# Loading a small residual in its final layout, and x in one transfer, in a single-core decode step

## The chip, the core and the metric

The kernel runs on one core of a Trainium2 chip. The metric is the device time of one execution in microseconds (us). A core has five engines that work side by side: TensorE (PE in the profile, with its weight loads as PEld), VectorE (DVE), ScalarE (ACT), GpSimd (POOL) and SyncE (SP). Each has its own queue of instructions, which it works off in order. Transfers between the memories are carried out by 16 DMA engines; an instruction on SP's or ACT's queue issues a transfer and is done, and a semaphore says later that the data have landed.

## What is computed

One decode step: a layer norm of x, grouped-query attention over the last 1024 cached positions, a gated feed-forward network on the same normalised x, and a residual.

```python
x = A_x                                   # (8, 1, 512) bf16: 8 sequences, one token each
xn = layernorm(x)
q = (xn @ wq)                             # 32 heads of 128; 8 key/value heads
p = softmax(q @ k_window.T * 128**-0.5)   # k_window, v_window: last 1024 of 4096 positions
s = (p @ v_window) @ wo                   # (8, 1, 512)
g = silu((gelu(xn @ w_gate) * (xn @ w_up)) @ w_down)
return x + s * g
```

Every key, value and weight is used once: per sequence 2 MB of keys and 2 MB of values, then 4 MB of wq, three feed-forward matrices of 1792 KB each and 4 MB of wo, all in bf16.

## The kernel before

All work is in one function, written so that each engine runs its instructions in the order of the text. The big transfers are all issued from SP: keys of sequence 0 (line 73, two transfers of 1 MB), wq (line 94, two of 2 MB), then keys and values of the other sequences in the order in which they are used, the feed-forward weights (lines 423 and 426) and wo (line 437), whose last megabyte is cut into pieces of 640, 256 and 128 KB. They land in a ring of eight slots of 4 MB, 32 KB per partition, so that SP runs ahead of the computation.

The start of the computation is the layer norm of x. x_sb holds the eight rows of x on eight partitions. It is loaded by four transfers of two rows each, issued from ACT (line 68). DVE takes the statistics (lines 129 and 131), ACT the square root (line 133), DVE the reciprocal and xhat (lines 134 and 136). TensorE turns xhat (line 151), and DVE writes the result four times into xnR (line 153), whose 32 columns per block hold the eight sequences at every fourth place. xnR is the stationary operand of the q projection (line 248) and, later, of the feed-forward matmuls (line 451).

The residual is needed at the very end, in the layout of the output: 128 partitions in four blocks of 32, block t with columns 128t to 128t + 127 of x, and inside a block the sequence b on partition 4b (RB = 4). To bring x into that layout, POOL builds a padded identity xpad (lines 116 and 117), TensorE multiplies it with the four column blocks of x_sb (line 156), and ACT copies the result from PSUM into x_res (line 163), which is fp32. After that ACT does nothing until the q projection has finished, when it copies q out of PSUM (line 258).

Then DVE turns keys (line 235), TensorE forms scores (line 296), DVE and ACT do the softmax (lines 306 to 318), TensorE the values (line 340), for one sequence after the other. At the end come the feed-forward network (lines 451 to 492) and the output projection (line 499), which runs as the pieces of wo land; DVE multiplies by the gate (y, line 507), adds x_res (out_sb, line 509), and SP stores the result (line 511).

The framework counts landed transfers on eight semaphores. The trace names the semaphore of each transfer: the eight are used in turn over SP's and ACT's transfers together, and a transfer that uses one again waits for the earlier transfer on it to land. So at most eight transfers are under way. SP's instruction waits where it stands, and all that SP issues after it waits behind it.

Of the kernel before, what the change touches and what calls it, by code (L numbers as in the profile page):

```python
# [8 lines left out]
ALU = mybir.AluOpType  # L9
AX = mybir.AxisListType  # L10
BF16 = mybir.dt.bfloat16
FP32 = mybir.dt.float32
# [4 lines left out]
RB = 4  # L17
# [4 lines left out]
def kernel(  # L22
# [13 lines left out]
    nc = tc.nc  # L36

    B, Sq, D = A_x.shape
# [7 lines left out]
    P = nc.NUM_PARTITIONS  # L46
# [7 lines left out]
    DT = D // 4  # L54
# [3 lines left out]
    keep = ctx.enter_context(tc.tile_pool(name="keep", bufs=1))  # L58
# [3 lines left out]
    def slot(name):  # L62
        return ring.tile([P, 2 * ROW], BF16, name=name, tag="slot")


    x_sb = keep.tile([B, D], BF16, name="x_sb")
    for r in range(0, B, 2):
        nc.scalar.dma_start(out=x_sb[r : r + 2], in_=A_x.flatten_outer_dims()[r : r + 2])

    def load_cache(cache, b, name):  # L70
        t = slot(name).rearrange("p (g x) -> p g x", g=NG)
# [20 lines left out]
    for i in range(2):  # L92
        t = slot("wq_sb").rearrange("p (k n) -> p k n", k=NK // 2)
# [9 lines left out]
        out=ident,  # L103
        in_=ident,
        compare_op=ALU.not_equal,
        fill=1.0,
        base=0,
        pattern=[[-1, P]],
        channel_multiplier=1,
# [2 lines left out]
    nc.vector.memset(eps_sb, 1e-5)  # L112
    xnR = keep.tile([P, NK, 4, 32], BF16, name="xnR")
    nc.vector.memset(xnR, 0.0)
    xpad = keep.tile([B, 32], BF16, name="xpad")
    nc.gpsimd.memset(xpad, 0.0)
    nc.gpsimd.affine_select(
        out=xpad,
        in_=xpad,
        compare_op=ALU.not_equal,  # L120
        fill=1.0,
        base=0,
        pattern=[[-1, 32]],
        channel_multiplier=RB,
    )


    stats = keep.tile([B, nc.vector.BN_STATS_DIM], FP32, name="stats")
    nc.vector.bn_stats(out=stats, in_=x_sb)  # L129
    mv = keep.tile([B, nc.vector.BN_AGGR_DIM], FP32, name="mv")  # L130
# [6 lines left out]
        out=xhat,  # L137
# [3 lines left out]
        op0=ALU.subtract,  # L141
        op1=ALU.mult,
    )
    x_res = keep.tile([P, DT], FP32, name="x_res")
    warm = keep.tile([B, 1], FP32, name="warm")
    nc.scalar.activation(out=warm, in_=rstd, func=ACT.Exp)
    with tc.tile_pool(name="ps_x", bufs=1, space=PSUM) as ps_x:
        xnT_ps = ps_x.tile([P, NK, B], BF16, name="xnT_ps")
        xv = xhat.rearrange("b (p k) -> b k p", k=NK)
        for k in range(NK):  # L150
            nc.tensor.transpose(xnT_ps[:, k, :], xv[:, k, :], ident[0:B, 0:B])  # L151
        for j in range(4):
            nc.vector.tensor_copy(out=xnR[:, :, j, 0 : RB * B : RB], in_=xnT_ps)
        xr_ps = ps_x.tile([P, DT], FP32, name="xr_ps")
        for t in range(4):
            nc.tensor.matmul(
                xr_ps[32 * t : 32 * t + 32, :],
                xpad,
                x_sb[:, t * DT : (t + 1) * DT],
                start=True,  # L160
                stop=True,
            )
        nc.scalar.copy(out=x_res, in_=xr_ps)

    qd = Hq // NG
    neg_st = consts.tile([P, 4, Hq], BF16, name="neg_st")
# [5 lines left out]
        out=hv,  # L174
        in_=hv,
        compare_op=ALU.not_equal,
        fill=0.0,
        base=0,
        pattern=[[0, 4 * NG], [-1, HG], [0, rep]],
        channel_multiplier=1,  # L180
    )
    nc.gpsimd.affine_select(
        out=neg_st,
        in_=neg_st,
        compare_op=ALU.is_ge,
        fill=0.0,
        base=HG - 1,
        pattern=[[0, 4 * Hq]],
        channel_multiplier=-1,
# [3 lines left out]
        out=neg_mv,  # L193
        in_=neg_mv,
        compare_op=ALU.not_equal,
        fill=1.0,
        base=0,
        pattern=[[0, 512 // HG], [-1, HG]],
        channel_multiplier=1,
# [7 lines left out]
    for g in range(NG):  # L207
        nc.vector.tensor_reduce(
            out=sel[:, g, g * qd : (g + 1) * qd],
            in_=ident.rearrange("p (t g h) -> p g h t", t=4, g=NG)[:, g],  # L210
# [5 lines left out]
        out=own, in_=ident.rearrange("p (i e) -> p e i", e=8), axis=AX.X, op=ALU.add  # L216
    )
    pick = consts.tile([P, 4 * NU], BF16, name="pick")
    with nc.allow_low_precision(reason="sums of zeros and a single one"):
        nc.vector.tensor_reduce(  # L220
            out=pick, in_=ident.rearrange("p (a e) -> p a e", e=8), axis=AX.X, op=ALU.add
# [22 lines left out]
    with tc.tile_pool(name="ps_q", bufs=1, space=PSUM) as ps_q:  # L244
        q_ps = [ps_q.tile([P, 512], FP32, name=f"q_ps{i}") for i in range(8)]
        for k in range(NK):
            for i in range(8):
# [4 lines left out]
                    start=(k == 0),  # L252
                    stop=(k == NK - 1),
# [174 lines left out]
    for u in range(NU):  # L428
        if u % 2 == 0:
            pair = slot("wo_sb").rearrange("p (v j d) -> p v j d", v=2, d=D)  # L430
        t = pair[:, u % 2]
# [15 lines left out]
    for n, ws in (("z_ps", wgu[0]), ("u_ps", wgu[1])):  # L447
        ps = ps_f.tile([P, FT], FP32, name=n)
        for k in range(NK):
            for t in range(4):  # L450
# [4 lines left out]
                    start=(k == 0),  # L455
                    stop=(k == NK - 1),
# [6 lines left out]
        out=z2, in0=z2, scalar1=0.044715, scalar2=1.0, op0=ALU.mult, op1=ALU.add  # L463
# [11 lines left out]
        out=hT.rearrange("p j b -> p (j b)"), in_=h_bf.rearrange("p (y j) -> p j y", j=NJ)  # L475
    )
    f_ps = ps_f.tile([P, DT], FP32, name="f_ps")
    for j in range(NJ):
        for t in range(4):
# [4 lines left out]
                start=(j == 0),  # L484
                stop=(j == NJ - 1),
# [4 lines left out]
        out=g_sb, in0=g_sb, scalar1=0.5, scalar2=0.5, op0=ALU.mult, op1=ALU.add  # L490
# [5 lines left out]
    for u in range(NU):  # L496
        for j in range(8):
            for t in range(4):
# [4 lines left out]
                    start=(u == 0 and j == 0),  # L503
                    stop=(u == NU - 1 and j == 7),
# [7 lines left out]
        out=out_f.rearrange("b (t d) -> t b d", t=4), in_=out_sb[0 : P : RB, :]  # L512
# [31 lines left out]
```

## Time and profile before

| What | Value |
|---|---|
| median of 3 runs | 121.49 us (121.39 to 121.63) |
| the profiled execution | 121.48 us, of which its span is 119.4 us |
| PE, DVE, ACT, POOL busy | 73.0, 75.8, 31.4, 3.2 us |
| mean granted TensorE clock | 0.838 |
| read from memory over the span | 47.46 MB, mean 399 GB/s with the write |
| DMA queue of SP (q1) | 6228 packets, 47.46 MB, 94.3% of 16 engines' span |
| DMA queue of ACT (q10) | 16 packets, 0.01 MB, 0.0% |
| idle of DVE until x has landed | 5.7 us |
| idle of ACT until q is ready (line 258) | 12.2 us |

The profile is one execution, seen by the hardware. The span runs from the first instruction to the last; what lies between it and the time of the run, some 2.1 us here, is before and after the program. The page cuts the span into 40 slices of about 3 us and gives the busy share of each engine and of the DMA engines in each. Beside the page, the trace has every instruction with its semaphores and every packet that a DMA engine moved, with its start, duration and size. Most packets of the large transfers are 8192 bytes and take 309 ns.

### The profile page before, as it was taken

To read this page: it belongs to the slowest core of one execution; us is meant where nothing else is said; L and a number is where in the kernel's file an instruction comes from. 1 tells how busy PE (TensorE), PEld (TensorE's weight loads), DVE (VectorE), ACT (ScalarE), POOL (GpSimd) and SP (SyncE) were. 2 spreads that over 40 slices of the span, in tenths; PEclk is the share of its full clock that TensorE was granted. 3 is DMA by queue.
4 is the path that set the end of the run, shared out by engine and by line. 5 is a ranking of instruction groups with operands and counts; after the bars stand their busy time and mean duration, and the time that the engine had idled before them with its cause. 6 is when DMAs were issued, how large, how long until landed. Compare 5 with 4: busy or idle time off the path is not lost.

```text
span 119.4 us, 2300 instructions
## 1 busy us (share of the span) xinstructions
PE 73.0 (61%) x985; PEld 38.7 (32%) x992; DVE 75.8 (63%) x101; ACT 31.4 (26%) x75; POOL 3.2 (3%) x10
## 2 busy tenths in 40 slices
PE   0001499811994987969687674991994547545370
PEld 0000134300341544535443351450453433143350
DVE  1048978399739999999959959909943241651000
ACT  2233000676007052341712510700616211200000
POOL 2006100000000000000000000000000000000000
PEclk9999999985599999999999998599589855555555
DMA  1999999999999999999999999999999999999930
GB/s 47 411 445 417 434 425 431 417 428 434 428 420 425 431 423 423 428 423 431 417 431 420 431 423 423 428 428 423 420 434 439 437 433 418 427 421 417 412 148 3
DMA packets 6254, 47.61 MB, mean 399 GB/s; under 512 B 732, under 2 KB 868, under 8 KB 1124
## 3 DMA queue, kind: packets, MB, share of 16 engines
q1 hardware_dynamic: 6228, 47.46, 94.3%
q8 instruction: 8, 0.13, 0.4%
q10 hardware_dynamic: 16, 0.01, 0.0%
q14 instruction: 2, 0.02, 0.0%
HBM read 47.46 MB, written 0.01 MB: 397 GB/s over the span
## 4 chain that ended last, share of the span: by engine, by line
DMA 85%; DVE 6%; PE 4%; SPq 2%; issue 1%
DMA k_sb<-in_A_k_cache_dram 48%; DMA wo_sb<-in_A_wo_dram 20%; DMA v_sb<-in_A_v_cache_dram 17%; DVE kT L235 4%; PE S_ps L296 2%; PE s_ps L499 1%; SPq L73 1%; DVE mx L306 1%; SPq L94 1%; PE O_ps L340 1%; PE r_ps L389 1%; DVE y L507 0%; DVE out_sb L509 0%; DVE oT L392 0%; DVE m L311 0%
## 5 line engine op out<-in xcount | busy, mean ns | idle before, releaser
L296 PE MATMUL S_ps<-kT,qbd 128*128 128x512 bf16 x128 | 34.1, 413 | 15.5 <-DVE kT L235 11.9
L235 DVE STREAM_TRANSPOSE kT<-k_sb 128x2048 int32<-128x2048 int32 x16 | 36.5, 2289 | 4.4 <-DMA k_sb<-in_A_k_cache_dram 4.3
L296 PEld LDWEIGHTS <-qbd 128*128 128x128 bf16 x128 | 12.8, 102 | 31.9 <-issue 16.4
L248 PE MATMUL q_ps<-wq_sb,xnR 128*128 128x512 bf16 x32 | 9.8, 481 | 4.3 <-DMA wq_sb<-in_A_wq_dram 4.3
L316 ACT ACTIVATE nb<-m 32x1 f32<-32x1 f32 x32 | 6.4, 201 | 22.5 <-DVE m L313 22.2
L306 DVE TENSOR_REDUCE mx<-S_ps 128x1 f32<-128x1024 f32 x8 | 9.6, 1196 | 4.1 <-PE S_ps L296 4.1
L318 ACT ACTIVATE P_sb<-S_ps,nb 128x1024 bf16<-128x1024 f32 x8 | 11.1, 1390 | 0.3
L340 PE MATMUL O_ps<-v_sb,pT 128*32 128x128 bf16 x512 | 9.1, 226 | 2.6 <-DVE pT L329 2.6
L340 PEld LDWEIGHTS <-pT 128*32 128x32 bf16 x512 | 7.6, 100 | 5.6 <-issue 3.0
L353 ACT COPY O_sb<-O_ps 128x256 f32<-128x256 f32 x8 | 3.0, 372 | 23.3 <-PE O_ps L340 23.3
L329 DVE STREAM_TRANSPOSE pT<-P_sb 128x512 int32<-128x512 int32 x8 | 5.7, 711 | 3.4 <-ACT P_sb L318 3.3
L248 PEld LDWEIGHTS <-xnR 128*128 128x128 bf16 x32 | 3.7, 118 | 10.1 <-issue 8.1
L361 PE MATMUL o_ps<-O_sb,sel 128*32 128x128 f32 x32 | 6.3, 332 | 0.9 <-ACT O_sb L353 0.9
L499 PE MATMUL s_ps<-wo_sb,oT 128*32 128x128 bf16 x128 | 4.4, 307 | 3.7 <-DMA wo_sb<-in_A_wo_dram 3.7
L258 ACT CAST q_both<-q_ps 128x512 bf16<-128x512 f32 x6 | 3.0, 611 | 12.2 <-PE q_ps L248 12.2
L151 PE MATMUL xnT_ps<-ident,xhat 8*128 8x8 bf16 x4 | 0.3, 174 | 8.9 <-DVE xhat L136 8.9
L499 PEld LDWEIGHTS <-oT 128*32 128x32 bf16 x128 | 3.5, 136 | 4.7 <-issue 4.5
L361 PEld LDWEIGHTS o_ps<-O_sb,sel 128*32 128x32 f32 x32 | 3.4, 128 | 5.0 <-issue 1.7
L507 DVE TENSOR_TENSOR y<-s_ps,g_sb 128x128 f32<-128x128 f32 x1 | 0.3, 292 | 7.2 <-PE s_ps L499 7.2
L285 PE MATMUL S_ps<-neg_mv,neg_st 128*128 128x512 bf16 x9 | 3.3, 384 | 1.9 <-DVE q_both L258 1.9
L129 DVE BATCH_NORM_STATS2 stats<-x_sb 8x6 f32<-8x512 bf16 x1 | 0.7, 681 | 5.7 <-DMA x_sb<-in_A_x_dram 5.7
L240 DVE MEMSET qbd<- 128x4096 uint32 x1 | 3.5, 3472 | 0.8 <-issue 0.8
(64 smaller groups left out, 51.2 us busy)
## 6 DMA issues: line engine op xcount, KB each, us to landing
k_sb<-in_A_k_cache_dram SPq DMA_DIRECT2D x16, 1024.0 KB, 19.7
v_sb<-in_A_v_cache_dram SPq DMA_DIRECT2D x16, 1024.0 KB, 20.0
wq_sb<-in_A_wq_dram SPq DMA_DIRECT2D x2, 2048.0 KB, 11.4
wo_sb<-in_A_wo_dram SPq DMA_DIRECT2D x3, 1024.0 KB, 25.1
wgu_sb<-in_B_w_gate_dram SPq DMA_DIRECT2D x1, 1792.0 KB, 21.4
wgu_sb<-in_B_w_up_dram SPq DMA_DIRECT2D x1, 1792.0 KB
wd_sb<-in_B_w_down_dram SPq DMA_DIRECT2D x1, 1792.0 KB
wo_sb<-in_A_wo_dram SPq DMA_DIRECT2D x1, 640.0 KB
```

Of the source, the lines that this page charges most:

```text
L235: nc.vector.transpose(out=t.bitcast(I32), in_=k_sb[b][:, g].bitcast(I32))
L240: nc.vector.memset(qbd, 0.0)
L248: nc.tensor.matmul(q_ps[i], xnR[:, k, :, :].rearrange("p j b -> p (j b)"), wq_sb[k][:, i * 512 : (i + 1) * 512], start=(k == 0), stop=(k = ...
L285: nc.tensor.matmul(S[b][:, half, :], neg_st.rearrange("p j h -> p (j h)"), neg_mv.rearrange("p a n -> p (a n)"), start=True, stop=False,)
L296: nc.tensor.matmul(S[b][:, half, :], qbd[:, m, b, w, g, :], kv[:, half * 16 : (half + 1) * 16, m, :, w], start=False, stop=(g == NG - 1 an ...
L306: nc.vector.tensor_reduce(out=mx, in_=S[b].rearrange("p a c -> p (a c)"), axis=AX.X, op=ALU.max)
L316: nc.scalar.mul(nb[32 * j : 32 * j + 32, :], m1, -inv)
L318: nc.scalar.activation(out=P_sb[b].rearrange("p c i w -> p c w i"), in_=S[b].rearrange("p a (c w i) -> p (a c) w i", w=2, i=32), func=ACT.Exp,
L329: nc.vector.transpose(out=pT[b].rearrange("p c h w -> p (c h w)").bitcast(I32), in_=P_sb[b].rearrange("p c i w -> p (c i w)").bitcast(I32),)
L340: nc.tensor.matmul(O_ps[b][32 * t : 32 * t + 32, g, :], pT[b][:, c // 2, :, c % 2], vv[:, c, :], start=(c < 4), stop=(c >= C - 4),)
L361: nc.tensor.matmul(o[:, 0:Dh], sel[:, g, :], O_sb[b][:, g, :], start=(g == 0), stop=(g == NG - 1))
L499: nc.tensor.matmul(s_ps[32 * t : 32 * t + 32, :], oT[:, j, u, :], wo[u][:, j, t * DT : (t + 1) * DT], start=(u == 0 and j == 0), stop=(u = ...
```

## The change

x is loaded in one transfer of eight rows. xpad, the four matmuls with it and ACT's copy are gone. x_res is now bf16; POOL fills it with zeros, and three transfers issued from ACT, after the activation `warm`, write x into it straight from memory: one of column blocks 0 and 1 (16 rows of 256 bytes), one of block 2 and one of block 3 (8 rows of 256 bytes each). DVE's addition at the end reads a bf16 operand in place of an fp32 one. Before and after there are four small transfers from ACT.

```diff
     x_sb = keep.tile([B, D], BF16, name="x_sb")
-    for r in range(0, B, 2):
-        nc.scalar.dma_start(out=x_sb[r : r + 2], in_=A_x.flatten_outer_dims()[r : r + 2])
+    nc.scalar.dma_start(out=x_sb, in_=A_x.flatten_outer_dims())
...
-    xpad = keep.tile([B, 32], BF16, name="xpad")
-    nc.gpsimd.memset(xpad, 0.0)
-    nc.gpsimd.affine_select(
-        out=xpad,
...
-        pattern=[[-1, 32]],
-        channel_multiplier=RB,
-    )
...
-    x_res = keep.tile([P, DT], FP32, name="x_res")
+    x_res = keep.tile([P, DT], BF16, name="x_res")
+    nc.gpsimd.memset(x_res, 0.0)
     warm = keep.tile([B, 1], FP32, name="warm")
     nc.scalar.activation(out=warm, in_=rstd, func=ACT.Exp)
...
-        xr_ps = ps_x.tile([P, DT], FP32, name="xr_ps")
-        for t in range(4):
-            nc.tensor.matmul(
-                xr_ps[32 * t : 32 * t + 32, :],
-                xpad,
-                x_sb[:, t * DT : (t + 1) * DT],
-                start=True,
-                stop=True,
-            )
-        nc.scalar.copy(out=x_res, in_=xr_ps)
+    x_t = A_x.flatten_outer_dims().rearrange("b (t d) -> t b d", t=4)
+    for a, z in ((0, 2), (2, 3), (3, 4)):
+        nc.scalar.dma_start(out=x_res[32 * a : 32 * z : RB, :], in_=x_t[a:z])
```

More of the change, by code (lines that the diff above doesn't have):

```diff
@@ L114 @@
     nc.vector.memset(xnR, 0.0)
-    xpad = keep.tile([B, 32], BF16, name="xpad")
-    nc.gpsimd.memset(xpad, 0.0)
-    nc.gpsimd.affine_select(
-        out=xpad,
[L119 to L122, printed above, removed]
-        pattern=[[-1, 32]],
-        channel_multiplier=RB,
-    )
     stats = keep.tile([B, nc.vector.BN_STATS_DIM], FP32, name="stats")
```

## The prediction

> **What bounds the kernel now.** I read the page's slices first.
>
> ```profile
> DMA  1999999999999999999999999999999999999930
> GB/s 47 411 445 417 434 425 431 417 428 434 428 420 425 431 423 423 428 423 431 417 431 420 431 423 423 428 428 423 420 434 439 437 433 418 427 421 417 412 148 3
> ```
>
> The DMA engines are full in every slice but the first and the last two, at some 425 GB/s, while no compute engine is over 63% busy. Second, the chain of waits in order of time, its end:
>
> ```profile
> 70.88 19.86 DMA v_sb<-in_A_v_cache_dram
> ...
> 90.76 24.04 DMA wo_sb<-in_A_wo_dram
> ...
> 114.84 1.28 PE s_ps L499 x28
> ...
> 116.15 0.30 DVE y L507
> ...
> 116.47 0.29 DVE out_sb L509
> ```
>
> Transfers make 85% of that chain; after the last one come a few matmuls, two DVE instructions and the store. Third, does SP ever issue too late? The waits of SP's queue:
>
> ```profile
> SPq L73 <- DMA k_sb<-in_A_k_cache_dram: 25.3, 13, 2.3
> SPq L73 <- DMA v_sb<-in_A_v_cache_dram: 19.2, 10, 2.5
> SPq L73 <- DMA wq_sb<-in_A_wq_dram: 8.5, 2, 4.3
> SPq L73 <- DVE oT L392: 0.3, 1, 0.3
> ```
>
> SP waits for earlier transfers to land (eight semaphores, eight transfers under way), and for compute once, 0.3 us, with some 20 us of transfers queued ahead. So the time is: when the stream starts, how long the slowest DMA engine needs, and the tail. From the packet records: the first key packet starts at 2.52 us, the last wo packet ends at 115.47, the last matmuls start at 115.80, out_sb ends at 116.76, the store lands at 118.26 and the span ends at 119.4. Fourth, the start, in the timeline:
>
> ```profile
> 0.80 1.54 ACTq L68 DMA_DIRECT2D x_sb<-in_A_x_dram  x4
> 0.80 1.30 SPq L73 DMA_DIRECT2D k_sb<-in_A_k_cache_dram  x2
> ...
> 7.02 0.68 DVE L129 BATCH_NORM_STATS2 stats<-x_sb 8x6 f32<-8x512 bf16 x1 [5.71 <-DMA x_sb<-in_A_x_dram]
> ...
> 9.13 0.29 PE L156 MATMUL xr_ps<-x_sb,xpad 8*32 8x128 bf16 x4
> 9.23 0.52 DVE L153 COPY xnR<-xnT_ps 128x32 bf16<-128x32 bf16 x4 [0.38 <-PE xnT_ps L151]
> ...
> 9.65 0.24 ACT L163 COPY x_res<-xr_ps 128x128 f32<-128x128 f32 x1
> ...
> 13.71 0.58 PE L248 MATMUL q_ps<-wq_sb,xnR 128*128 128x512 bf16 x1 [4.29 <-DMA wq_sb<-in_A_wq_dram]
> ```
>
> x is late (7.02), but xnR is ready at 9.75 and the q projection starts at 13.71, when wq lands. The layer norm has 3.96 us to spare.
>
> **x in one transfer.** The first of the four x transfers, issued at 0.80, ran its packets at 1.74 and 1.79, before any key packet, and its semaphore was full at 2.34. The other three waited behind key packets (starts 3.69 to 6.17). One transfer in the first one's place should land near 2.4, some 4.5 us earlier; three issues (0.24, 0.40 and 0.28 us of ACT) go. Statistics, xhat and xnR move up to about 5 us, and DVE's first key transposes from 11.68 to some 8.1, when the first keys have landed. What hides all of it is the 4.29 us wait for wq. Value: 0. A gain of 4.5 us would need that wait to go; the transfer that it waits for does not move.
>
> **The matmuls, xpad and the copy.** 0.29 us of PE, 0.24 of ACT, 0.12 and 0.21 of POOL, all before 9.9 us and all under the same wait: 0. The zeroing of x_res is a POOL memset, between 0.10 us (the constant memsets) and DVE's 0.17 for a 128x128 bf16 tile, on a POOL that idles 8.2 us after that: 0.
>
> **ACT's three new issues.** At 0.24 to 0.54 us each (the four at line 68) they take 0.7 to 1.6 us, from about 5.2 us on. Behind them on ACT is the copy of q, for which ACT sat idle 12.2 us until 22.09. Eight semaphores go round over both queues, so an issue of ACT can also wait for an earlier transfer. Four small transfers before, four after: later in the kernel the turn is as it was. SP, which had to wait for the x transfers' semaphores (its issues at 3.33, 6.80, 7.45 and 8.11), will stand instead on a wq or x_res transfer until about 13 or 18 us; 9 or 10 MB have been issued by then and 4 or 5 are still to come (2.45 us each MB, so 10 us or more), and the stream does not run dry. If ACT is held until wq has landed (SP was held so until 13.59 and 18.42), q's copy is still in time. Value 0; up to 3.7 us late (a wait for values landing near 25.8) it is still covered, since the first slot that depends on it, that of the values of sequence 0, was refilled at 46.4 and free some 4.8 us earlier.
>
> **The packets in the stream.** This is the only place where microseconds can come from. Packets on one DMA engine run one after the other: each x row took 46 ns and each semaphore write 9, and the next key packet started right behind. The engines do not end together. By the ends of the wq transfers (12.55 to 13.23) they are up to 0.68 us apart, and these offsets stay to the end, except where an instruction fetch of 16 KB runs on one engine, which sets it back by 1.42. The last engine is one with 0.37 at the start and a fetch at 83.4: 1.79. The two engines with x packets stand at 0.11 and 0.15; the first gets a fetch and ends at 1.52. So the x packets that go, 3 x (46 + 9) = 0.17 us on each, are not on the engine that ends last: 0, in bounds of 0 to -0.17. The x_res packets: if block 0-1 goes to two engines as the pairs of x rows did, each takes 8 packets, and one or two more of the other transfers. The nearest row is the store of the output, 32 packets of 256 bytes at 15 to 18 ns: 10 x 18 + 3 x 9 = 0.21, against the 0.17 that goes: 1.56, still under 1.79. On other engines up to 2 x (18 + 9) = 0.05. I take +0.05. The bound above is the 60 ns of the slowest x row in the stream: 10 x 60 + 27 - 165 = 0.46 more, 1.98, which is 0.19 over 1.79.
>
> [...] The x rows in the trace held their engine for some 46 ns, so the sum here counts packets alone.
>
> **The start of the stream.** The windows by stage:
>
> ```profile
> 2.70:5.20 2.50, 0.00 (x0) 0.00 (x0) 0.00 (x0) 0.95 (x1) 0.00 (x0) 1.00 0.89 368
> 5.20:7.70 2.50, 0.00 (x0) 0.00 (x0) 0.68 (x1) 0.00 (x0) 0.00 (x0) 1.00 1.04 437
> 30.00:60.00 30.00, 25.25 (x296) 12.70 (x299) 26.24 (x24) 10.08 (x27) 0.00 (x0) 0.95 1.01 425
> ```
>
> The last two numbers are the DMA engines' busy share and GB/s. Between 2.7 and 5.2 the share is 0.89: several engines stood idle for 0.16 to 0.42 us near 4.8, among them the one that ends last. The queued x issues may be what held their descriptors up, or it is chance. If all such gaps went, the last engine would stand near 0.1 + 1.42, so -0.25; a start of the keys earlier than 2.52 (they start 1.72 us after the issue, the output store 1.30) could give up to -0.4. In the other direction, the fetch can meet an engine with 0.68 in place of 0.37: +0.31. I take -0.1, nearer to nothing, as no row ties the gaps to x.
>
> **The tail.** out_sb adds a bf16 operand: 128 elements at 0.29 us either way. It may need two extra semaphore instructions (21 and 50 ns at line 129), which run while y is busy: 0, at most +0.07.
>
> Sum: 0.05 - 0.1 = -0.05 on 121.48 is 121.43; I say 121.4. The profiled execution is 0.01 below the median, so nothing is added.
>
> **The rivals.** First, faster by the start: gaps gone (-0.25) and the keys up to 0.15 earlier, 121.1. For it: the 0.89 share, and x transfers that queue among key packets. Against it: SP's issues at the start took 0.58 to 0.66 us, and 0.60 at 6.8, when ACT issued nothing. Second, slower by the small packets: they cost 60 ns each on the engine that also gets a fetch, +0.19, and the tail +0.07: 121.75. It decides from some 40 ns a packet. For it: rows of 256 bytes written at stride four beside the stream. Against: 15 to 18 ns in the store. Third, x does move the end: all compute 4.5 us earlier would give 117; against it stand the waits of SP, which are for transfers. Fourth, the x transfer does not go first and x is as late as now: then the prelude stays, and the time is that of my forecast.
>
> **How the numbers follow.** No measurable change, from 121.25 to 121.7: 0.46 (the fourth included). Faster by the start: 0.31, the third 0.01. Slower by packets or by a worse meeting of fetch and engine: 0.22. A measurement of this kernel can tell 0.2% (0.24 us) from no change. That gives 0.32, 0.46 and 0.22. The range, 121.0 to 121.8, holds the first rival's time and the second's. The likeliest case's own is 121.25 to 121.7.
>
> **What would show it.** x landed near 2.4 us and statistics before 3; the q projection still at 13.7, released by wq; three x_res issues on ACT near 5 us or held there; 425 GB/s in the middle; the last wo packet within 0.3 of 115.5. The forecast is wrong if the DMA share falls in a middle slice, if q starts later than 13.7, or if out_sb stands apart from y.

## The result, and the profile after

The changed kernel takes 123.09 us (median of 5 runs, 122.91 to 123.49), against 121.49 us (121.39 to 121.63) before: a ratio of 1.0137, with a 95% interval of 1.0116 to 1.0158. The forecast was 121.4 with a range up to 121.8, so it was 1.7 us too low; a slower kernel had a chance of 0.22. The profiled execution ran 123.49 us, the longest of the five, but its span of 120.9 is like the others' (120.8 to 121.0), and spans are compared below.

The page's slices of the changed kernel:

```profile
DMA  2999999999999999999999999999999999999930
GB/s 76 390 454 430 418 417 420 426 420 426 420 423 420 412 420 420 426 409 423 420 417 415 423 423 417 417 423 423 420 423 438 413 442 413 419 413 423 396 121 3
```

The DMA engines are as full as before, from the first slice to the last. But the second row is lower in 28 of the 40 slices and higher in 8: the same engines, never idle, move less. A window shows it best. This is the stretch from 30 to 60 us of the changed kernel (start and end, length, busy time and count of PE, PEld, DVE, ACT and POOL, then PE's clock, the DMA share and GB/s):

```profile
30.00:60.00 30.00, 25.25 (x296) 12.70 (x299) 26.23 (x24) 10.08 (x27) 0.00 (x0) 0.95 1.01 420
```

Every compute engine has the same figures as before within 0.01 us, the clock is the same 0.95, and the last number is 420 where it was 425. That is 1.2% of everything that still has to be loaded.

The start of the changed kernel, from its timeline:

```profile
0.81 0.59 ACTq L67 DMA_DIRECT2D x_sb<-in_A_x_dram  x1
...
2.40 0.68 DVE L115 BATCH_NORM_STATS2 stats<-x_sb 8x6 f32<-8x512 bf16 x1 [1.08 <-DMA x_sb<-in_A_x_dram]
...
3.83 1.34 ACTq L143 DMA_DIRECT2D x_res<-in_A_x_dram  x2
...
4.61 0.52 DVE L140 COPY xnR<-xnT_ps 128x32 bf16<-128x32 bf16 x4 [0.38 <-PE xnT_ps L138]
...
5.21 0.63 ACTq L143 DMA_DIRECT2D x_res<-in_A_x_dram  x1
...
13.64 9.94 PE L226 MATMUL q_ps<-wq_sb,xnR 128*128 128x512 bf16 x32 [9.06 <-DMA wq_sb<-in_A_wq_dram]
```

What the change is about worked: x is there 4.6 us earlier, xnR at 5.13 in place of 9.75. The q projection starts at the same time as before, because it waits for wq, now for 9.06 us in place of 4.29. And the end, from the chain of waits in order of time:

```profile
91.80 24.37 DMA wo_sb<-in_A_wo_dram
...
116.22 1.32 PE s_ps L477 x26
...
117.56 0.30 DVE y L485
117.86 0.04 DVEq L487
117.90 0.04 issue
117.94 0.29 DVE out_sb L487
```

The span grew by 1.47 us. In the records of the packets the last one of wo ends at 116.72 in place of 115.47: 1.25 us. From there to y it is 0.84 us in place of 0.68: 0.16. From y to out_sb it is 0.38 in place of 0.32 (the row DVEq is a semaphore instruction that waits for x_res): 0.06. After that nothing differs.

### The profile page after: what moved, and what is told of

The parts are those of the page before. It is cut to its first block, busy times and chain, and to the rows that moved or that the text cites. A ratio compares the mean times of both kernels' runs of the same rounds, so it can differ in the third digit from the quotient of the medians.

```text
span 120.9 us, 2285 instructions
## 1 busy us (share of the span) xinstructions
PE 73.5 (61%) x981; PEld 38.6 (32%) x988; DVE 75.9 (63%) x101; ACT 31.2 (26%) x74; POOL 3.0 (3%) x9
## 4 chain that ended last, share of the span: by engine, by line
DMA 85%; DVE 6%; PE 4%; SPq 2%; issue 1%; DVEq 0%
DMA k_sb<-in_A_k_cache_dram 48%; DMA wo_sb<-in_A_wo_dram 20%; DMA v_sb<-in_A_v_cache_dram 16%; DVE kT L213 4%; PE S_ps L274 2%; PE s_ps L477 1%; SPq L72 1%; DVE mx L284 1%; SPq L93 1%; PE O_ps L318 1%; PE r_ps L367 1%; DVE oT L370 0%; DVE y L485 0%; DVE out_sb L487 0%; DVE m L289 0%
## 5 line engine op out<-in xcount | busy, mean ns | idle before, releaser
L274 PE MATMUL S_ps<-kT,qbd 128*128 128x512 bf16 x128 | 35.2, 423 | 16.5 <-DVE kT L213 12.9
L213 DVE STREAM_TRANSPOSE kT<-k_sb 128x2048 int32<-128x2048 int32 x16 | 36.5, 2288 | 5.2 <-DMA k_sb<-in_A_k_cache_dram 5.2
L339 PE MATMUL o_ps<-O_sb,sel 128*32 128x128 f32 x32 | 5.5, 297 | 1.0 <-ACT O_sb L331 1.0
L236 DVE CAST q_both<-q_ps 128x512 bf16<-128x512 f32 x2 | 1.3, 671 | 7.0 <-PE q_ps L226 7.0
L458 PE MATMUL f_ps<-wd_sb,hT 128*32 128x128 bf16 x56 | 1.7, 312 | 3.2 <-DVE hT L452 3.2
```

The source lines that it names most:

```text
L213: nc.vector.transpose(out=t.bitcast(I32), in_=k_sb[b][:, g].bitcast(I32))
L236: e(out=q_bf[:, i * 512 : (i + 1) * 512], in_=q_ps[i])
L274: nc.tensor.matmul(S[b][:, half, :], qbd[:, m, b, w, g, :], kv[:, half * 16 : (half + 1) * 16, m, :, w], start=False, stop=(g == NG - 1 an ...
L339: nc.tensor.matmul(o[:, 0:Dh], sel[:, g, :], O_sb[b][:, g, :], start=(g == 0), stop=(g == NG - 1))
```

## The experiments

**Where the 1.25 us are.** In the packet records, the median key or value packet of 8192 bytes takes 309 ns in every part of the kernel before, and from 16 us on over 99% of them take at most 310. In the changed kernel nearly nine in ten still take 309 at 16 to 19 us; from 23 us on most take 312, and one in five 317 or more. Between 30 and 92 us the mean is 313.7, against 309.0 before (without the six or seven packets of some 3170 that took over 400 ns). The landing of 1 MB then takes 2.486 us in place of 2.453. The packets of 14,336 bytes of the feed-forward weights go from 535 to mostly 538 or 545, a mean of 4.6 ns more, about as much for nearly twice the bytes, so it is a cost for each packet. All 16 engines have it, also the eight that no x_res packet went to: of the 49 packets that start between 26 and 27 us none takes 310 ns or less.

Three theories. B, the nearest to the forecast's slow rival: the 256-byte packets leave the DMA engines slower. C: SP's order of issue is different, since SP now stands on wq and x_res semaphores. A came from the list of tile addresses of the two compiled programs. Tiles are laid one after the other in each partition: x_sb and the small tiles, then qbd and others, then the ring, then kT. The xpad tile takes 64 bytes of a partition, x_res 512 as fp32 and 256 as bf16. So the change moved everything behind them down by 64 + 256 = 320 bytes, and the ring's begin from byte 55296, which is 108 x 512, to 54976, which is 192 past a multiple of 256. (A slot of the ring takes 16 KB of each partition, 2 MB in all, and not the 32 KB and 4 MB of the description above; both are multiples of 256, so all eight slots are off by the same.) A says that each packet into such a place costs more. To move the ring alone, an unused tile is put ahead of it:

```diff
     two = ctx.enter_context(tc.tile_pool(name="two", bufs=2))
+    gap = ctx.enter_context(tc.tile_pool(name="gap", bufs=1))
+    gap.tile([P, 160], BF16, name="gap_sb")      # 320 bytes
     ring = ctx.enter_context(tc.tile_pool(name="ring", bufs=N_SLOTS))
```

**The changed kernel with the ring back in its place.**

> The changed kernel with 320 unused bytes per partition ahead of the ring, so that the ring of eight slots begins again at byte 55296 of a partition (a multiple of 512), in place of 54976 (192 past a multiple of 256). Theory A (the address: transfers into slots that do not begin on such a multiple take longer for each packet): the median packet of 8192 bytes goes back from 312 to 309 ns in the middle of the run, the time to 121.3 to 121.7 us. Theory B (the 256-byte packets of the three x_res transfers leave the DMA engines slower): nothing changes, 312 ns and 123.1. Theory C (SP's order of issue, held by the semaphores of wq and x_res): 123.1 too.

Measured: 121.50 us, ratio to the kernel before 1.0001 (0.9988 to 1.0013), and packets of 309 ns. Its window from 30 to 60 us:

```profile
30.00:60.00 30.00, 25.49 (x300) 12.52 (x297) 24.60 (x24) 10.09 (x27) 0.00 (x0) 0.94 1.01 426
```

All of the loss is gone with the whole change in the kernel, x_res packets and SP's new order included. B and C fall.

**The kernel before with the ring moved.** The same gap tile, of 96 bf16 elements, in the kernel before.

> The kernel before, with 192 unused bytes per partition ahead of the ring: it begins at 55488, as far past a multiple of 256 as in the changed kernel; kT, which lies behind the ring, moves as well. Theory A: packets of 312 ns from some 20 us on and 122.9 to 123.2 us, without any part of the change. B and C: 121.5.

Measured: 122.88 us, ratio 1.0111 (1.0097 to 1.0125). Its window:

```profile
30.00:60.00 30.00, 25.48 (x322) 12.88 (x324) 25.60 (x24) 10.09 (x27) 0.00 (x0) 0.98 1.01 419
```

A kernel without a line of the change has its slow stream, with the same median of 312 ns, mean of 313.7 and 2.486 us a MB, and the same 0.83 us from the last packet to y.

**The ring alone.** One question was left in that: kT moved too, and DVE and TensorE work on it. A second gap behind the ring puts kT back on a multiple of 512:

```diff
+    gap2 = ctx.enter_context(tc.tile_pool(name="gap2", bufs=1))
+    gap2.tile([P, 160], BF16, name="gap2_sb")
     kT_pool = ctx.enter_context(tc.tile_pool(name="kT_pool", bufs=3))
```

> As the last one, with 320 more unused bytes behind the ring, so that kT is on a multiple of 512 again and only the ring is off. Theory A, with the DMA writes as the cause: 122.9 to 123.2, as the last one. If it is the engines' accesses to kT that cost (theory D): 121.5. B and C: 121.5.

Measured: 122.92 us, ratio 1.0113 (1.0098 to 1.0128), 419 GB/s in the same window and the same packets as the last kernel. It is the place where the ring begins. DVE and TensorE read from the ring too, so their reads have moved with it; that these are not the cause is shown with the first 20 us below.

**How far off, and from which multiple.** The kernel before with gaps of 32, 64, 128 and 256 bytes:

> The kernel before with 32 unused bytes ahead of the ring (begin 55328, 32 past a multiple of 256). A1 (each packet that does not begin on a multiple of 256 costs one extra step on the write side, however far off it is): 122.9 us, as with 192. A2 (the cost grows with the bytes past the multiple, 1.35 us at 192): 121.7.

> 64 unused bytes. A1: 122.9 us. A2: 122.0. A3 (only multiples of 64 matter): 121.5, which the 192 of the earlier run speaks against.

> 128 unused bytes. A1: 122.9 us. A2: 122.4. A4 (multiples of 128 are enough): 121.5.

> 256 unused bytes (begin 55552, a multiple of 256 and not of 512). A1 and A2: 121.5 us. A5 (multiples of 512 are needed): 122.9.

| ring begins past a multiple of 256 by | run | ratio (95% interval) | mean packet of 8192 bytes, 30 to 92 us |
|---|---|---|---|
| 0 (256 more than before) | 121.57 us | 1.0006 (0.9997 to 1.0015) | 309.0 ns |
| 32 | 123.36 us | 1.0151 (1.0137 to 1.0165) | 314.5 ns |
| 64 | 122.83 us | 1.0110 (1.0097 to 1.0124) | 313.6 ns |
| 128 | 122.59 us | 1.0089 (1.0075 to 1.0103) | 313.2 ns |
| 192 (the second run above) | 122.88 us | 1.0111 (1.0097 to 1.0125) | 313.7 ns |

The windows of the gaps of 32 and of 256:

```profile
30.00:60.00 30.00, 25.52 (x301) 12.63 (x300) 26.33 (x24) 10.08 (x27) 0.00 (x0) 0.95 1.01 419
```

```profile
30.00:60.00 30.00, 25.47 (x301) 12.75 (x300) 26.36 (x24) 10.08 (x27) 0.00 (x0) 0.95 1.01 426
```

The multiples of 256 that the ring began at are free (309.0 ns and 1.0006 at 55552), and 512 is not needed. Off them there is a step of about 1.1 us or more (A1), but it is not quite the same everywhere, and it does not grow with the bytes past the multiple (A2): 64 and 192 cost the same, 32 clearly the most, and 128 the least by its packets, though its time is hardly clear of that of 64. In these points it goes by the largest power of two that the address is a multiple of (32; 64; 128); no further address was tried.

**The parts of the change, with the ring in its place.** x in one transfer alone, in the kernel before (the residual by matmuls; the ring did not move):

> The kernel before with x in one transfer alone: the four matmuls, xpad and the copy stay, and the ring stays at 55296. Theory A: 121.4 to 121.6, 309 ns. Theory B: 121.5, as the small packets are not there. Theory C: the turn of the semaphores shifts by three, so SP's issues move; a change of up to 1 us either way would speak for it.

Measured: 121.69 us, ratio 1.0014 (1.0004 to 1.0025). Then the residual by three transfers alone, with the gap of 320 bytes:

> The residual by three transfers alone: x still comes in four transfers, and 320 unused bytes bring the ring back to 55296. With theory A settled, what is left of the change: 121.4 to 121.6 us if the small packets cost nothing on the path (my sum: 0.05), 121.7 to 121.8 if they sit on the engine that ends last.

Measured: 121.90 us, ratio 1.0029 (1.0015 to 1.0044). And the changed kernel with a gap of 64 bytes, the size of xpad, in place of 320:

> The changed kernel with 64 unused bytes alone, the size of the xpad tile that went: the ring begins at 55040, a multiple of 256 and not of 512. If multiples of 256 are all that counts: 309 ns and 121.4 to 121.6 us. If the changed kernel needs the old address for another reason: above 122.5.

Measured: 121.75 us, ratio 1.0026 (1.0007 to 1.0045); packets of 309 ns. The four kernels that hold the change or a part of it, with the ring on a multiple of 256, lie between 1.0001 and 1.0029, both parts together being cheapest in one and not in the other. The last three came out 0.1 to 0.3 us above the 121.4 to 121.6 that was expected. The spans of all executions are closer for the whole change: their medians are 119.4 and 119.55 us, against 119.4 and 119.5 of the kernel before beside them; each part alone has a longer one, 119.6 and 119.9. What the parts cost beside the address is therefore open between nothing and about 0.35 us, and is no gain in any of them. In the three with x_res transfers out_sb starts 0.38 us after y, as in the changed kernel, in place of 0.32; where the rest lies was not settled.

**Why the first 20 us look free.** In the two kernels with the ring 192 bytes off and in the changed kernel most packets are as fast as ever at first, and the share of longer ones grows from some 18 to some 28 us (in the changed kernel the share of at most 310 ns is 0.89 at 16 to 19 us, 0.58 at 19 to 23 and 0.07 at 23 to 28). If each packet owes some 4 ns and an engine can put that off until it owes the time of some 50 packets (0.2 us, an estimate from some 16 us of packets of 309 ns), a hole in the stream should wipe the debt out. The loads of one turn of the loop are moved behind a small copy, so that the queue runs empty (the tile `held` takes 64 bytes ahead of the ring, and the gap tile is chosen so that the ring begins where the expectations say):

```diff
-        if b + 2 < B:
+        if b + 2 < B and b != 3:
             load_k(b + 2)
         if b + 1 < B:
-            load_v(b + 1)
+            if b != 3:
+                load_v(b + 1)
...
         keep_o(b)
+        if b == 3:
+            held = keep.tile([P, 16], FP32, name="held")
+            nc.sync.dma_start(out=held, in_=O_sb[b][:, 0, 0:16])
+            load_k(b + 2)
+            load_v(b + 1)
```

> The kernel before with the ring at 55488 (192 past a multiple of 256) and a hole in the stream: the loads of sequence 3's turn in the loop are issued only when a small copy out of O_sb of sequence 3 has been issued, so the queue runs empty once near the middle. Theory P1 (each packet into such a slot owes some 4 ns on the write side, which a DMA engine can hide until about 0.2 us are owed): after the hole, packets take 309 ns again for some 30 to 60 packets on each engine, 8 to 15 us, and 312 and more after that. Theory P2 (the cost sets in with the program's time or with the count of transfers): 312 from the first packets after the hole on.

> The same hole with the ring at 55808, a multiple of 512. P1 and P2: 309 ns before and after the hole. The difference of this kernel to the last one is what the address costs with the hole: under P1 a little less than the 1.3 us without one (two stretches of some 12 to 20 us are free in place of one), about 1.1; under P2 1.3.

Measured: 129.77 us and 129.45 us, one run each, with a hole of 4.1 and 4.7 us near 60 us. The windows of the first (ring at 192) ahead of the hole, behind it, and later; then the same of the second (ring on a multiple):

```profile
30.00:56.00 26.00, 22.20 (x280) 11.21 (x283) 22.87 (x21) 7.83 (x21) 0.00 (x0) 0.96 1.01 420
66.00:78.00 12.00, 7.89 (x97) 3.90 (x98) 8.46 (x10) 2.62 (x7) 0.00 (x0) 0.72 1.00 421
82.00:98.00 16.00, 12.29 (x109) 5.53 (x108) 9.23 (x8) 4.48 (x12) 0.00 (x0) 0.74 1.01 418
```

```profile
30.00:56.00 26.00, 22.18 (x277) 11.03 (x280) 21.68 (x20) 7.84 (x21) 0.00 (x0) 0.93 1.01 425
66.00:78.00 12.00, 7.80 (x93) 3.86 (x93) 8.11 (x8) 2.42 (x7) 0.00 (x0) 0.63 1.00 421
82.00:98.00 16.00, 13.02 (x166) 6.55 (x169) 10.62 (x12) 4.87 (x13) 0.00 (x0) 0.80 1.01 425
```

Ahead of the hole and late the two differ by 5 and 7 GB/s; right behind it not at all. The packet records say the same: with the ring off, the share of packets of at most 310 ns is 0.03 to 0.12 in slices of 4 us from 28 to 56 us, 0.85 and 1.00 in the two slices from 68 to 76 us, 0.67 in the next, and 0.03 to 0.12 from 80 us on. With the ring on a multiple it is 0.81, 1.00, 1.00 and 0.99 in these slices behind the hole. P1's course holds, about 15 us of free packets as it says, and P2 falls. The difference of the two times, 0.32 us, is smaller than the 1.1 that P1 asked for. But the holes are not equally long: from the last packet ahead of the hole to the copy's first it is 4.1 us with the ring off and 4.7 without, and to the next keys 4.9 and 5.5. The span is 0.39 us longer with the ring off, so without this difference of 0.56 the address costs 0.95 us, near the 1.1; these are single runs.

The trace also shows the debt itself. Behind its data each DMA engine writes a packet of 4 bytes to the transfer's semaphore (692 of them on SP's queue in the kernel before, with a median of 9 ns). The time from the end of that packet's record to the semaphore's update, as a median in ns over the packets of SP's queue:

| kernel | 4 to 7 us | 12 to 14 | 17 to 19 | 30 to 56 | 63 to 67 | 67 to 72 | 75 to 80 |
|---|---|---|---|---|---|---|---|
| before | 345 | 319 | 332 | 325 | 328 | 326 | 331 |
| before, ring 192 off | 337 | 377 | 416 | 455 | 454 | 455 | 451 |
| the same with the hole at 59 to 63 us | 349 | 381 | 415 | 459 | 330 | 361 | 451 |

So the first 20 us are not free: each update comes later and later behind its packet, by some 0.13 us in the end, less than the 0.2 us reckoned; from then on the packets themselves are longer. A hole wipes the debt out, and it grows again. All the kernels with the ring off stand at 448 to 473 ns from 30 to 56 us, and all with it on a multiple at 323 to 331. It begins before anything reads the ring: in the kernels with four x transfers DVE's first key transpose starts at 11.68 us or later, and between 7 and 11.6 us the time is already 336 to 358 ns with the ring off, against 303 to 314 on a multiple. Nor do DVE's reads from the ring take longer off it: a key transpose takes 2288 ns there and 2289 before. That leaves the writing, by the author's estimate.

## Why the prediction was wrong

**The step that failed** is the one headed "The matmuls, xpad and the copy", with the sum "0". It priced xpad's instructions and the zeroing of x_res, and no step priced what xpad and x_res occupy. Two small tiles that shrink or go, 320 bytes of each partition, moved the eight slots of the ring that 47 MB are written to. Its place in the sum was 0; measured, the address alone costs 1.35 us in the kernel before (0.0111 of 121.5), and putting the ring back returns the whole 1.6 us that the change lost.

**The bound was read rightly and one part of it was taken for a constant.** The forecast said that the time is the start of the stream, what the slowest engine needs, and the tail. That is what the 1.47 us of span are made of. It took the 425 GB/s of the middle for given. It named that rate as a sign of being right, and the last wo packet within 0.3 us of 115.5 as another; both failed (420 GB/s, 116.72). But as a sign of being wrong it named the DMA share, which stayed full, and it had no rival in which the rate falls for all engines.

**The slow rival had the direction and not the cause.** It asked for 60 ns a packet for the 256-byte transfers. They took 15 to 18 ns, as the store did in the kernel before, and 16 of them went to two engines, as was worked out, the last at 14.54 us; and with the ring in its place the kernel with all of them is at 1.0001.

**What held.** x landed near 2.4 us (statistics at 2.40, forecast "before 3"), the q projection still waited for wq and started at 13.64; SP stood on the wq transfers until 13.52 and 18.4, as reckoned, and the stream did not run dry (a DMA share of 1.00 from 13.7 to 20 us). ACT's three issues ran from 3.83 to 5.84, earlier than the 5.2 forecast, since two of them went while the table load ahead of `warm` ran, and took 0.63, 0.68 and 0.63 us each, where 0.24 to 0.54 was said; ACT's next work, the copy of q, came at 22.10, and SP stood 0.3 us on an x_res transfer. The tail's extra semaphore instruction was put at 0 with a bound of 0.07, and cost 0.06: the wait does not run wholly beside y. And out_sb did stand apart from y, as the forecast's last sign of being wrong has it, by these 0.06 us.

**The start of the stream** gained a little and it did not reach the end. The DMA share between 2.7 and 5.2 us, on which the forecast leaned, went from 0.89 to 0.97; over all the profiles it is 0.90 to 0.97 with one x transfer and 0.84 to 1.00 with four, so it says nothing about x. The distance between the engines does. At the end of the first wq transfer they are 0.30 to 0.55 us apart in the four profiles with one x transfer and 0.68 to 0.95 in the ten with four, and the last engine ends it at 12.90 to 13.12 us in place of 13.23 to 13.41. The forecast's -0.1 is what that engine gained in the changed kernel (13.12 in place of 13.23). Yet with the ring on a multiple the last wo packet ends at 115.42 to 115.59 with one x transfer and at 115.47 to 115.68 with four, no clear gain; why it is lost on the way was not followed up. The late first key packet of the kernel before, 2.52, has nothing to do with x: in all other profiles, with one x transfer or four, it starts at 2.24 to 2.26.

**What is shown and what is not.** That the place where the ring begins decides is shown from both sides (the changed kernel with the ring put back, the kernel before with the ring moved), as is the multiple (the four gaps), and that the cost can be put off and sets in again (the two kernels with the hole). That the debt stands behind the packet's record is shown by the updates that fall behind (336 to 358 ns in place of 303 to 314) while nothing reads the ring yet; that it is on the way into SBUF is the author's estimate from that. The tail agrees, where the last packet's record ends 0.83 to 0.86 us ahead of y in every kernel that is off and 0.68 to 0.76 in those on the multiple. What on that way takes the time is not shown. Why 32 is dearer than 64 was not tried. No run here was faster than the kernel before; the best form of the change only equals it.

## What to carry to other kernels

In a kernel bound by its transfers, look up where the big buffers begin in a partition after every change of a small tile, and keep them on a multiple of 256 bytes, where the packets here kept their 309 ns; one tile of 64 or 320 unused bytes is worth 1.3 to 1.6 us, more than anything that the change set out to move. When a change removes or shrinks a tile, its bytes are a step of their own: what stands behind it moves. And a stream that is as busy as before but moves less per second is to be followed into single packets, early ones and late ones apart, since here nearly nine in ten packets at 16 to 19 us still took 309 ns, and only the semaphores' updates told of the cost.

## What the runs showed of the hardware

- A transfer into SBUF places that begin off a multiple of 256 bytes took longer for each row: 4.2 to 5.5 ns for rows of 8192 bytes, by the mean packets above (1.4 to 1.8% of 309 ns), and 4.1 to 5.6 ns for rows of 14,336 bytes (535.0 to 539.1 to 540.6).
- For some 20 us of a full stream, and for some 15 us again after a hole of 4 us, that cost hardly showed in the packets (0.89 of those at 16 to 19 us took at most 310 ns in the changed kernel; 0.85 and 1.00 in the two slices from 68 to 76 us behind the hole); in that time the semaphores' updates fell behind the packets, from some 0.33 us to some 0.46.
- Eight rows of 1 KB, issued ahead of the bulk at 0.81 us, had been moved by 2.06 and their semaphore was full at 2.37; 32 rows of 256 bytes, issued into a full stream between 3.83 and 5.84 us, were moved between 8.3 and 14.55, and the last semaphore was full at 15.61.
